# Replacing a fixed stage order by a list scheduler, with one pool of PSUM banks and smaller first loads

## The chip, the cores and the metric

One core of a Trainium2 chip. The metric is the time on the device in microseconds (us) of one execution. Five instruction queues matter: TensorE (PE in the profile, its weight loads as PEld), VectorE (DVE), ScalarE (ACT), GpSimd (POOL, which here mostly issues loads) and SyncE (SP, which issues the stores).

Two things about the times have to be known from the start. First, the profile records the clock that was *granted* to TensorE, as a share of full speed. It is either 1.0 or 0.5, and it changes several times in one execution. Second, the changes fall on a grid of 3.41 us whose phase against the kernel is chance. On one core the states "fast" and "slow" of a run only say whether it was within 1.5% of the fastest of its kernel. The mean clock that is quoted for a run or a stretch counts the time before the run's first clock record as full clock. Ratios called "ratio of the fast runs" are the mean time of one kernel's fast runs over that of the other's of the same rounds, so they are not quite the ratio of the medians that are quoted beside them.

## The reference, cut to what matters

Eight batches of eight heads, 576 tokens, 64 wide. Four heads see the last 32 tokens, four see every fourth of the last 128. The result goes through a soft mixture of experts: every token has logits for 32 slots, softmax over tokens builds the slot inputs, 8 experts of two layers work on 4 slots each, softmax over slots brings the result back.

```python
scores = np.where(masks, scale * q @ k.T, -1e9); attn = softmax(scores) @ v   # local windows
x = attn.transpose(0, 2, 1, 3).reshape(4608, 512)
logits = x @ phi                                   # 4608 x 32
slot_input = softmax(logits, axis=0).T @ x         # 32 x 512, over all tokens of all batches
slot_out[e] = relu(slot_input[e] @ w1[e]) @ w2[e]  # needs every batch
out = softmax(logits, axis=1) @ slot_out           # 4608 x 512, f32
```

The experts need all batches, so the program has three main parts in a row: attention with routing (batch by batch), experts, output.

## The kernel before

A "group" is the four heads of one type in one batch: 16 groups. The stages of a group, by the letters that the code and this text use:

- A: 4 pieces of 18 transposes of q, k, v (96x64 blocks) into one PSUM bank; ScalarE copies Q, K, V out of it.
- B: 6 transposes of v back to token order; VectorE copies.
- S: 6 score matmuls (4 pieces per group); ScalarE takes exp, VectorE multiplies by the mask.
- P: 12 matmuls of probabilities with v (2 pieces); VectorE divides by the row sum into XB.
- once per batch: X (4 pieces of 6 transposes of XB), L (8 logits matmuls of 288 columns), exp on ScalarE, E (12 small matmuls of 32 columns), I (48 small matmuls of 32 columns that sum up the slot inputs).

```python
    ps2 = [A(nc.psum_tensor(f"ps2_{i}", [128, 2, 512], F32)) for i in range(2)]   # two pairs of banks
    ps1 = [A(nc.psum_tensor(f"ps1_{i}", [128, 512], F32)) for i in range(3)]      # three single ones
    psA = A(nc.psum_tensor("psA", [128, 512], F32))                               # the slot sums
    # ... each stage takes the next buffer of its ring
    def st_A(g, r):
        # ...
                    i_ = t.transpose(pbf[64 * hx:64 * hx + 64, NR * i:NR * i + NR],
                                     stg_x[s][0:NR, 2 * typ + hx, c, :], ident[0:NR, 0:NR])
    # ...
    for step in range(-1, 2 * B + 2):     # the fixed order; g = step, b = g // 2, odd = g % 2
        if on: st_B(g, 0); st_S(g, 0, 0)
        if nx: st_A(g + 1, 0)
        if on: st_S(g, 0, 1)
        if nx: st_A(g + 1, 1)
        if pr: st_P(g - 1, 1)
        if on: st_B(g, 1)
        if odd and 0 <= b - 1 < B: st_L(b - 1)
        if not odd and 0 <= b - 1 < B: st_X(b - 1, 2); st_X(b - 1, 3)
        if on: st_S(g, 1, 0)
        if nx: st_A(g + 1, 2)
        if odd and 0 <= b - 1 < B: st_E(b - 1)
        if on: st_S(g, 1, 1)
        if nx: st_A(g + 1, 3)
        if on: st_P(g, 0)
        if odd and 0 <= b - 1 < B: st_I(b - 1)
        if odd and 0 <= b < B: st_X(b, 0); st_X(b, 1)
        # ... then the loads of batch b + 3 and of one expert's weights
```

Loads: `load_w1(0)`, then q, k, v of batch 0 for all eight heads, and so on in turn, all from GpSimd's queue.

The softmax here doesn't subtract the row's maximum and nothing guards it: scores larger than these inputs give would overflow.

## Time and profile before

261.67 us median of 2 runs (261.45 to 261.89); the profiled run has a span of 261.6 us.

| stretch | us | TensorE busy | idle |
|---|---|---|---|
| wait for the first q, k, v | 0 to 17.8 | 0 | 17.8 |
| attention and routing | 17.8 to 217.5 | 184.0 | 15.7 |
| experts | 217.5 to 235.0 | 15.2 | 2.3 |
| output | 235.0 to 261.6 | 10.5 | (stores) |

The table comes from this view, the busy time of each engine by stretch. Each line has the stretch in us from the start, its length, then the busy us of PE, PEld, DVE, ACT and POOL with the instruction counts, the mean granted clock, the DMA engines' share and GB/s:

```profile
0.00:17.80 17.80, 0.03 (x2) 0.06 (x3) 0.63 (x10) 1.28 (x1) 14.95 (x41) 1.00 0.91 175
17.80:217.50 199.70, 184.03 (x2848) 150.62 (x2848) 105.09 (x202) 110.84 (x280) 15.69 (x28) 0.64 0.72 142
217.50:235.00 17.50, 15.22 (x174) 7.31 (x173) 2.66 (x7) 1.05 (x3) 0.00 (x0) 0.87 0.00 1
235.00:261.60 26.60, 10.51 (x35) 2.14 (x36) 12.71 (x18) 12.06 (x18) 0.00 (x0) 0.77 0.89 355
```

Attention is bound by TensorE: 92% busy, the others near 55%. But the mean clock of 0.64 is still too kind, as the slice view shows. It cuts the span in 40 slices; PE and DMA are busy tenths, PEclk the granted clock in tenths:

```profile
PE   0027998999899989989998999899888758888700
...
PEclk9999999997557555555575575555555555999955
DMA  6999999999999509998910664178037700007998
```

The nines of PEclk in the first nine slices are an absence of records: the first clock record of this trace is at 58.4 us. What TensorE's clock was is better read from durations. This is the timeline of TensorE alone (start, us, line, operation, tile written <- tiles read, shapes, count), around one of the short spells of full clock, which the records put at 82.27 to 85.68 us:

```profile
83.23 0.57 PE L307 MATMUL ps_1<-ident,stg 96*64 96x96 bf16 x18
83.74 0.73 PE L377 MATMUL ps_0<-VN,PT 128*96 128x65 bf16 x12
84.39 1.63 PE L457 MATMUL psA<-ET,XB 96*64 96x32 bf16 x48
...
89.23 0.93 PE L307 MATMUL ps_0<-ident,stg 96*64 96x96 bf16 x18
90.09 1.17 PE L377 MATMUL ps_1<-VN,PT 128*96 128x65 bf16 x12
...
203.52 1.63 PE L457 MATMUL psA<-ET,XB 96*64 96x32 bf16 x48
```

The same piece A (L307) takes 0.57 us in the spell and 0.93 us outside it; P (L377) takes 0.73 and 1.17 us. Before 58 us they take 0.93 and 1.17 us too, so the clock was at half there. I (L457, 48 matmuls of 32 columns) takes 1.63 us at either clock: at 84.39 us in the spell and at 203.52 us far outside one.

What TensorE waited for, longest first (us in total, times, longest):

```profile
PE ps_0 L307 <- DMA stg<-in_v_dram: 17.8, 1, 17.8
PE ps_1 L398 <- DVE XB L386: 3.3, 4, 1.3
PE ps_1 L333 <- ACT VT L318: 2.6, 4, 1.9
```

### The profile page before, as it was taken

The numbers are of one execution on the slowest core, as the hardware profiler recorded it, in microseconds if no ns is written. First come the engines' busy times: TensorE is split into PE (matmuls) and PEld (weight loads), VectorE is DVE, ScalarE is ACT, GpSimd is POOL, SyncE is SP. The second block draws the span as 40 slices with busy tenths as digits, with TensorE's granted clock in tenths as the row PEclk, the third lists the DMA queues.
The fourth block names the chain that finished last, engine by engine and source line by source line (L and its number), as shares of the span: only waits on it lengthen the run. The fifth ranks groups of instructions, "written<-read, shape, count | busy, mean of one in ns | idle before, by whom it ended". The sixth has DMA issues, their size and how long they took to land.

```text
span 261.6 us, 7056 instructions
## 1 busy us (share of the span) xinstructions
PE 209.8 (80%) x3055; PEld 160.1 (61%) x3056; DVE 121.1 (46%) x237; ACT 125.2 (48%) x302; POOL 30.6 (12%) x68
## 2 busy tenths in 40 slices
PE   0027998999899989989998999899888758888700
PEld 0025787778787867877787878778766734531100
DVE  0001557636644565466366545644664521219900
ACT  1017785565576545645655764456463010008900
POOL 7970300300030022002000000000000000000000
PEclk9999999997557555555575575555555555999955
DMA  6999999999999509998910664178037700007998
GB/s 110 207 219 208 220 209 217 214 215 212 219 198 216 118 4 189 220 219 153 215 37 3 114 113 99 19 148 147 18 38 137 152 0 3 3 0 289 406 404 345
DMA packets 8910, 40.88 MB, mean 156 GB/s; under 512 B 1456, under 2 KB 1456, under 8 KB 6832
## 3 DMA queue, kind: packets, MB, share of 16 engines
q0 software_dynamic: 5760, 30.94, 60.4%
q1 hardware_dynamic: 3120, 9.50, 9.2%
q8 instruction: 24, 0.39, 0.6%
q14 instruction: 6, 0.05, 0.0%
HBM read 61.93 MB, written 9.44 MB: 273 GB/s over the span
## 4 chain that ended last, share of the span: by engine, by line
PE 60%; ACT 10%; DMA 10%; DVE 9%; issue 4%; POOL 2%; POOLq 0%; ACTq 0%
DMA stg<-in_v_dram 10%; PE ps_1 L377 5%; PE psA L457 5%; PE ps_0 L377 4%; PE ps_2 L307 4%; PE ps_0 L307 4%; PE ps_1 L307 3%; PE ps_1 L587 3%; PE ps_0 L352 3%; PE ps_1 L417 3%; PE ps_0 L417 3%; DVE XB L386 3%; DVE w1r L612 3%; PE ps_1 L352 3%; ACT PT L358 3%
## 5 line engine op out<-in xcount | busy, mean ns | idle before, releaser
L307 PE MATMUL ps_0<-ident,stg 96*64 96x96 bf16 x414 | 21.2, 280 | 17.8 <-DMA stg<-in_v_dram 17.8
L358 ACT ACTIVATE PT<-ps_0 128x576 bf16<-128x576 f32 x32 | 21.1, 660 | 26.8 <-PE ps_0 L352 26.7
L358 ACT ACTIVATE PT<-ps_1 128x576 bf16<-128x576 f32 x32 | 21.1, 660 | 25.3 <-PE ps_1 L352 25.3
L361 DVE TENSOR_TENSOR PT<-PT,mask_d 128x576 bf16<-128x576 bf16 x32 | 14.7, 458 | 37.4 <-ACT PT L358 37.4
L307 PEld LDWEIGHTS ps_0<-ident,stg 96*64 96x64 bf16 x414 | 17.0, 162 | 20.7 <-POOL siT L293 17.7
L361 DVE TENSOR_TENSOR PT<-PT,mask_p 128x576 bf16<-128x576 bf16 x32 | 14.7, 458 | 25.8 <-ACT PT L358 25.1
L307 PE MATMUL ps_2<-ident,stg 96*64 96x96 bf16 x396 | 19.8, 275 | 0.2 <-DMA stg<-in_v_dram 0.2
L318 ACT ACTIVATE QT<-ps_0 128x288 bf16<-128x288 bf16 x23 | 10.4, 451 | 18.6 <-PE ps_0 L307 18.6
L377 PE MATMUL ps_1<-VN,PT 128*96 128x65 bf16 x192 | 17.8, 262 | 0.4 <-ACT PT L358 0.4
L377 PE MATMUL ps_0<-VN,PT 128*96 128x65 bf16 x192 | 17.8, 263 | 0.0
L307 PEld LDWEIGHTS ps_2<-ident,stg 96*64 96x64 bf16 x396 | 15.9, 159 | 3.1 <-issue 0.3
L377 PEld LDWEIGHTS ps_1<-VN,PT 128*96 128x96 bf16 x192 | 15.7, 183 | 2.3 <-PE ps_0 L352 0.6
L307 PE MATMUL ps_1<-ident,stg 96*64 96x96 bf16 x342 | 17.0, 274 | 0.0
L337 DVE COPY VN<-ps_1 128x768 bf16<-128x768 bf16 x12 | 6.6, 548 | 22.1 <-PE ps_1 L333 22.1
L377 PEld LDWEIGHTS ps_0<-VN,PT 128*96 128x96 bf16 x192 | 15.8, 184 | 1.6
L386 DVE TENSOR_TENSOR XB<-ps_0,RV 96x768 bf16<-96x768 f32 x16 | 15.3, 954 | 0.6
L386 DVE TENSOR_TENSOR XB<-ps_1,RV 96x768 bf16<-96x768 f32 x16 | 15.3, 953 | 0.6
L226 POOL DMA_DIRECT2D stg<-in_q_dram x8 | 4.4, 553 | 93.1 <-PE ps_1 L307 39.5
L307 PEld LDWEIGHTS ps_1<-ident,stg 96*64 96x64 bf16 x342 | 13.6, 158 | 2.4
L457 PE MATMUL psA<-ET,XB 96*64 96x32 bf16 x384 | 13.0, 217 | 0.6 <-DVE ET L443 0.6
L352 PE MATMUL ps_0<-QT,KT 64*128 64x96 bf16 x192 | 13.3, 267 | 0.0
L352 PE MATMUL ps_1<-QT,KT 64*128 64x96 bf16 x192 | 13.3, 267 | 0.0
(114 smaller groups left out, 377.8 us busy)
## 6 DMA issues: line engine op xcount, KB each, us to landing
out_dram<-w1r SPq DMA_DIRECT2D x18, 512.0 KB, 5.1
w1r<-in_moe_w_dram POOLq DMA_DIRECT2D x8, 1024.0 KB, 21.3
stg<-in_moe_w_dram POOLq DMA_DIRECT2D x6, 1024.0 KB, 8.0
stg<-in_q_dram POOLq DMA_DIRECT2D x8, 576.0 KB, 12.7
stg<-in_k_dram POOLq DMA_DIRECT2D x8, 576.0 KB, 14.8
stg<-in_v_dram POOLq DMA_DIRECT2D x8, 576.0 KB, 17.0
w2r<-in_moe_w_dram POOLq DMA_DIRECT2D x2, 1024.0 KB, 21.7
phi_st<-in_moe_phi_dram SPq DMA_DIRECT2D x1, 64.0 KB, 2.0
```

Of the source, the lines that this page charges most:

```text
L307: i_ = t.transpose(pbf[64 * hx:64 * hx + 64, NR * i:NR * i + NR], stg_x[s][0:NR, 2 * typ + hx, c, :], ident[0:NR, 0:NR])
L318: op("act", lambda ac, d=d, t=t: ac.activation(d, pv[:, t], ACTF.Copy), r=[pb], **{"w" if r == 0 else "a": [bd[par]]})
L337: op("dve", lambda vv: vv.tensor_copy(vt[:, half, :, :, 0:64], pbf[:, 0:768].rearrange("p (m x d) -> p m x d", m=NB, x=2)), r=[pb], w=[vb[ ...
L352: i_ = t.matmul(sc[:, hx, QB * mm:QB * mm + QB], KT[par][64 * hx:64 * hx + 64, half, QB * m:QB * m + 128], QT[par][64 * hx:64 * hx + 64, h ...
L358: op("act", lambda ac: ac.activation(pt[:], sc[:, :, 0:3 * QB], ACTF.Exp, scale=SCALE), r=[scb], w=[ptb])
L361: op("dve", lambda vv: vv.tensor_tensor(pt[:], pt[:], mk.unsqueeze(1).to_broadcast([128, 2, 3 * QB]), AluOp.mult), r=[b_mask[typ]], w=[ptb])
L377: i_ = t.matmul(po[0:QB, hx, 65 * m:65 * m + 65], pts[m // 3][0][:, hx, QB * (m % 3):QB * (m % 3) + QB], vt[:, half, m, hx, 0:65], start=T ...
L386: op("dve", lambda vv: vv.tensor_tensor(xd, pv[:, :, :, 0:64], rv[:].unsqueeze(3).to_broadcast([QB, 2, NB, 64]), AluOp.mult), r=[pob, rvb] ...
L417: i_ = t.matmul(lg[:, hf, 0:288], phi_pad[:, c].rearrange("p j i -> p (j i)"), XT[:, c, 288 * hf:288 * hf + 288], start=c == 0, stop=c == 3)
L457: i_ = t.matmul(psA[64 * typ:64 * typ + 64, 32 * c:32 * c + 32], x_, et[:, NB * typ + m, :], start=(b == 0 and m == 0 and c == 0), stop=(b ...
L587: i_ = t.matmul(sp_[32 * j:32 * j + 32, :], hT[:, hi, cc, j, :], w2v[e][:, cc, :], start=(hi == 0 and cc == 0), stop=(hi == 1 and cc == 7))
L612: op("dve", lambda vv, o=o, po=po: vv.tensor_scalar(ost[:, o % NO, 1, :], po[:, 1, :], rtok[:, 2 * o + 1:2 * o + 2], None, op0=AluOp.mult) ...
```

## The change

The intent: let a program, not a person, decide the order. Every operation becomes a task with an engine, an assumed duration and a due time. A list scheduler places tasks one by one: per engine it takes those that could start within 0.14 us of the earliest, and of those the one due first. The durations given for TensorE are those of the full clock (0.5 us for a piece A that takes 0.86 at half). PSUM becomes one pool of seven banks that the scheduler hands out. Loads are by four heads, and those of batch 0 go ahead of all weights. The setup memsets move from GpSimd to VectorE. The matmuls, evictions and bytes are the same.

```diff
+def place(tasks, banks, filler):
+    # ... ready lists per engine, bank occupancy, modelled start times
+            for t in lst:
+                st = t0
+                for p in t.preds:
+                    # ...
+                    st = max(st, p.end + lat)
+                for h in t.ps:
+                    if h.banks is None:
+                        f = find(h)              # a free bank, or two neighbours
+                        # ...
+                        st = max(st, f[0])
+                if e == "pe" and t.mode != last_mode[0]:
+                    st += 0.13
+                cands.append((st, t))
+            m = min(c[0] for c in cands)
+            st, t = min((c for c in cands if c[0] <= m + 0.14), key=lambda c: (c[1].due, c[1].idx))
 # ...
-    ps2 = [A(nc.psum_tensor(f"ps2_{i}", [128, 2, 512], F32)) for i in range(2)]
-    ps1 = [A(nc.psum_tensor(f"ps1_{i}", [128, 512], F32)) for i in range(3)]
+    NBK = 7
+    psum = A(nc.psum_tensor("psum", [128, NBK, 512], F32))
     psA = A(nc.psum_tensor("psA", [128, 512], F32))
 # ...
+        for typ in range(2):                      # loads by groups of four heads
+            for t, src in enumerate((q, k, v)):
+                load(lambda g, t=t, src=src, typ=typ: g.dma_start(
+                    stg[32 * t:32 * t + 32, s, 4608 * typ:4608 * typ + 4608].rearrange(...),
+                    src[b, 4 * typ:4 * typ + 4].rearrange(...)), due, 1.45, s_in[s][typ], ...)
 # ...
-        op("pe", pe, r=[b_id, b_in[s]], w=[pb])
+        op("pe", pe, r=[b_id, b_in[s][typ]], ps=[h], dur=0.5, due=due, mode="col")
 # ... every other stage likewise: a duration and a due time; I in two halves
-    for step in range(-1, 2 * B + 2):
-        # ... the fixed order
+    plan = {0: [("w1", 0)], 1: [("w1", 1)], 2: [("w1", 2)], 3: [("w1", 3)], 4: [("w1", 4)],
+            5: [("w1", 5), ("w1", 6)], 6: [("w1", 7), ("w2", 0), ("w2", 1)],
+            7: [("w2", e) for e in range(2, 8)]}
+    for b in range(B):
+        load_qkv(b, -26.0 + b)
+        # ... weights by plan, then the stages of both groups, then X, L, E, I
 # ...
+    for t in place(tasks, NBK, filler):
+        emit(t)
```

## The prediction

> **What bounds the kernel now.** Four stretches, read from the timeline and the stretch table.
> (a) 0 to 17.8 us: TensorE waits for the first batch of q, k, v (waits by engine: 17.8 us on the DMA of v), because 1 MB of w1 and all eight heads are queued ahead; the DMA engines moved about 213 GB/s.
> (b) 17.8 to 217.5 us: attention and routing. TensorE is the limit: 183.9 us busy of 199.7, while ScalarE and VectorE are near 60%. A batch takes 23.4 to 24.8 us, of which TensorE is idle only 1.1 to 1.3 us. The idle time is 9.0 us between 34 and 206 us; the rest is the first fill and the last batch's serial chain (idle 5.9 us from 196 to 218).
> (c) 217.5 to 235 us: the expert layers.
> (d) 235 to 261.6 us: 9.4 MB of output at 350 to 400 GB/s, DMA bound; the evictions keep 0.73 us per 512 KB, faster than the DMA.
>
> TensorE runs at half clock in most of (b). The slice table's 0.9 before 58 us only means that there is no record: 18 input transposes take 0.86 us there, 0.50 us at the full clock. The clock rose four times, each time after a window holding the logits matmuls (8 of 288 columns, about 1.95 us), and fell one window (3.4 us) later. The Trainium skill, "TensorE: Matmul & The Clock Gate", Part 4, says that transposes do not count as busy for the clock; the trace agrees: 104.5 to 129.3 us was 96% busy at clock 0.50.
>
> **What the change does.** The same matmuls, evictions and bytes. The order comes from a scheduler whose durations are those of the full clock (0.50 us for the transposes that take 0.86). Setup memsets move from GpSimd to VectorE. Banks 2x2+3 become a pool of seven. The first loads are half size and precede w1.
>
> **Costs on the critical path.**
> - Start: 0.88 MB instead of 2.8 MB before the first transpose: 4.2 us at 213 GB/s instead of 13.3; TensorE starts at 8.3 us instead of 17.8: -9.5.
> - Idle in (b): 15.9 us falls to about 8 (first fill 2, final chain 4.5, rest 1.5): -8.
> - TensorE's 183.9 us of work stays: the clock stays half for most of it, because the work that counts stays about a third of each window. A few more logits windows may warm: -2, with mode switches equal (six score matmuls of 41 ns hold 0.35 us, so about 0.1 each; the skill's "TensorEngine Tiling (Array Packing)", Tiling Modes, says that a mode change drains the engine).
> - Expert layers: row sums leave the path: -0.5. Output: unchanged.
> - More and smaller DMAs: GpSimd issues 24 more of 0.55 us, hidden. Loads need about 145 us and fit.
>
> Sum with the cold clock: 261.7 - 20 = 242. If the denser order keeps the clock full for most of attention (my chance: one in five), TensorE drops to about 6.5 us per group, the bound becomes ScalarE (7 to 8 us per group) and the loads, and the time falls to 195 to 215 us. Between both I put 238 us, range 212 to 248. Chances: faster 0.95, same 0.04, slower 0.01.
>
> **What would show it.** First transpose at 8 to 9 us; TensorE over 96% busy between 15 and 190 us; transposes still 0.86 us for 18; clock records mostly 0.5 with short spells of 1.0; expert layers begin near 198 us; output 25 us long and DMA bound.
>
> **What would make it wrong.** The clock staying full (much faster). The order, planned with half the real TensorE times, making engines wait in order for late work. More mode switches from finer interleaving. The second batch's load arriving late, since the pool of loads is in order.

## The result, and the profile after

214.32 us median of 2 runs (213.49 and 215.16); ratio of the fast runs 0.8397, with an interval of 0.8231 to 0.8563. Six more runs on another chip gave 214.36 us (210.93 to 216.56). The kernel before was unlucky in its first two runs: in 29 later ones it took 244.7 to 263.1 us (mean clock of the whole run from 0.83 down to 0.68). Where both ran, the medians were 255.54 and 214.36 us, a ratio of 0.839. The fast runs alone (2 of 11, and 3 of 6) have means of 244.75 and 212.8 us, a ratio of 0.87.

The same view by stretch, with the borders of the new kernel:

```profile
0.00:9.20 9.20, 0.00 (x0) 0.01 (x1) 4.81 (x31) 1.28 (x1) 7.87 (x19) 1.00 0.77 135
9.20:167.20 158.00, 139.38 (x2884) 117.13 (x2884) 99.76 (x203) 109.83 (x280) 28.23 (x53) 0.89 0.94 191
167.20:185.20 18.00, 15.08 (x138) 6.59 (x138) 2.27 (x6) 1.04 (x3) 0.00 (x0) 0.83 0.01 2
185.20:211.80 26.60, 9.82 (x35) 2.60 (x36) 11.94 (x18) 10.69 (x18) 0.00 (x0) 0.79 0.89 355
```

The start is 8.6 us shorter and the attention stretch 41.7 us; experts and output have not moved. The gain in attention is not idle time: idle is 18.6 us (158.0 less 139.4) against 15.7 before. It is TensorE's busy time, 139.4 us against 184.0, for the same 3055 matmuls of the whole program (36 row-sum matmuls of the expert part now fall in this stretch).

```profile
PE   0279999997899899799888999977946788899000
...
PEclk9999999999979999859998569997875569999955
DMA  5999999999999999999999998976940000069998
```

The first clock record is now at 36.8 us and says 1.0, and the nines of the middle are real. The timeline of TensorE shows it, cold at 26.7 and warm at 45 us:

```profile
26.70 1.17 PE L524 MATMUL psum<-VN,PT 128*96 128x65 bf16 x12
...
42.77 1.63 PE L619 MATMUL psA<-ET,XB 96*64 96x32 bf16 x48
...
45.37 0.57 PE L446 MATMUL psum<-ident,stg 96*64 96x96 bf16 x18
45.87 0.73 PE L524 MATMUL psum<-VN,PT 128*96 128x65 bf16 x12
```

And what TensorE waited for:

```profile
PE psum L446 <- DMA stg<-in_v_dram: 9.2, 1, 9.2
PE psum L446 <- issue: 2.9, 4, 1.3
PE psum L524 <- DVE PT L505: 2.5, 5, 1.8
PE psum L496 <- ACT KT L456: 1.6, 1, 1.6
```

The clock is not up all the time: the records of attention show spells of 20.5, 27.3, 20.5, 20.5 and 6.8 us at 1.0, with 3.4 to 10.2 us at 0.5 between them. So the question is why the clock is up so much longer, and whether that is all.

### What a window has to hold

The records change only on the 3.41 us grid, so each window can be set against the clock of the next. I counted the matmul work in each window as its moving columns at 2.4 GHz, whatever the clock really was (2.4 GHz is from the Trainium skill, "TensorE: Matmul & The Clock Gate", Part 1; the trace agrees: logits matmuls of 288 columns start 240 ns apart at half clock, that is, 1.2 columns per ns). A matmul that fills only 64 rows or 64 columns of the array (A, S, I) counts half; that weight is an assumption, chosen because it fits. Every matmul counts, transposes too. This is worked out from the trace, not a view of the profile; us of counted work by stage:

```
kernel  window  clock  work  next  of which
before   55.0   0.5    1.60  1.0   A .28 B .24 L .96 S .12
before   58.4   1.0    1.23  0.5   A .44 E .16 I .18 P .32 S .12
before   78.9   0.5    1.44  1.0   A .36 L .96 S .12
before   82.3   1.0    1.25  0.5   A .36 E .16 I .28 P .33 S .12
after    33.4   0.5    1.42  1.0   A .05 B .64 S .24 X .48
after    36.8   1.0    2.18  1.0   A .66 L .96 P .43 S .12
after    40.2   1.0    1.36  1.0   B .32 E .16 I .19 P .22 S .24 X .24
after    43.6   1.0    1.84  1.0   A .58 B .32 I .13 P .32 S .24 X .24
after    47.0   1.0    1.70  1.0   A 1.38 P .32
after    50.4   1.0    2.26  1.0   A .78 B .64 S .36 X .48
after    53.8   1.0    1.39  0.5   A .86 L .08 P .32 S .12
```

Over the 98 whole windows of attention in both traces, the rule "the next window is at full clock if this one holds 1.44 us of counted work" is wrong 10 times. Left out of the count, transposes make it wrong 21 times at the best line. The window at 33.4 us holds 24 transposes of B and X, 12 score matmuls and next to nothing else, and the clock rose. With its 1.42 us it is itself one of the 10 windows that the rule gets wrong, as is the one at 40.2 us, which kept the full clock with 1.36 us: near the line the rule doesn't decide. The halving carries much of it. In a recount of all the traces (575 windows after a first record, each matmul put into the window in which it starts), the best line with the halving is wrong 48 times. With every matmul counted whole it is wrong 143 times, no better than saying "as this window" (140).

By this count the old order at half clock stays under the line, and a denser order can stay over it. A batch holds 8.8 us of counted work (my sum over its stages). At half clock the old kernel needs 24.8 us for a batch, 1.21 us per window, which is under the line, so only a window that catches L whole rises. In the changed kernel a batch of 15.4 to 20.4 us (from L to L in the profiled run, all but the last; the clock is at 0.72 to 1.0 in them) holds 1.48 to 1.95 us per window on average, over the line. In the old order the window after each rise was the one with E and I, 1.22 to 1.26 us in all four spells, and it always fell back. In the first spell of the changed kernel the scheduler has S, B, X and S between E (40.9 us) and I (42.8 us), and L is followed by A and P at once.

Theory ("clock"): the order earns the clock, and the clock is the gain. Rival ("order"): the order, the pool of banks or the loads save time themselves, and the clock only follows.

### The profile page after: what moved, and what is told of

The parts are those of the page before. It is cut to its first block, busy times and chain, and to the rows that moved or that the text cites. A ratio compares the mean times of both kernels' runs of the same rounds, so it can differ in the third digit from the quotient of the medians.

```text
span 211.8 us, 6954 instructions
## 1 busy us (share of the span) xinstructions
PE 164.3 (78%) x3055; PEld 126.3 (60%) x3056; DVE 118.8 (56%) x258; ACT 122.8 (58%) x302; POOL 36.1 (17%) x71
## 4 chain that ended last, share of the span: by engine, by line
PE 54%; DVE 15%; ACT 14%; issue 6%; DMA 3%; POOL 1%; DVEq 0%; POOLq 0%
PE psum L446 9%; PE psum L524 7%; PE psum L470 6%; PE psum L496 6%; PE psA L619 6%; DVE w1r L762 5%; PE psum L551 5%; PE psum L574 5%; PE psum L734 4%; ACT QT L456 4%; ACT KT L456 3%; PE psum L679 3%; DMA stg<-in_v_dram 3%; ACT VT L456 3%; DVE XB L536 3%
## 5 line engine op out<-in xcount | busy, mean ns | idle before, releaser
L502 ACT ACTIVATE PT<-psum 128x576 bf16<-128x576 f32 x64 | 42.5, 675 | 26.3 <-PE psum L496 25.1
L446 PE MATMUL psum<-ident,stg 96*64 96x96 bf16 x1152 | 38.3, 232 | 12.2 <-DMA stg<-in_v_dram 9.2
L446 PEld LDWEIGHTS psum<-ident,stg 96*64 96x64 bf16 x1152 | 33.3, 129 | 15.7 <-issue 13.7
L456 ACT ACTIVATE QT<-psum 128x288 bf16<-128x288 bf16 x64 | 30.8, 482 | 11.9 <-PE psum L446 11.9
L456 ACT ACTIVATE VT<-psum 128x288 bf16<-128x288 bf16 x64 | 31.1, 488 | 1.3 <-PE psum L446 1.3
L536 DVE TENSOR_TENSOR XB<-psum,RV 96x768 bf16<-96x768 f32 x32 | 30.5, 954 | 1.1
L456 ACT ACTIVATE KT<-psum 128x288 bf16<-128x288 bf16 x64 | 31.0, 484 | 0.0
L524 PE MATMUL psum<-VN,PT 128*96 128x65 bf16 x384 | 26.8, 227 | 3.4 <-DVE PT L505 2.5
L524 PEld LDWEIGHTS psum<-VN,PT 128*96 128x96 bf16 x384 | 24.1, 144 | 6.4 <-DVE PT L505 3.6
L474 DVE COPY VN<-psum 128x768 bf16<-128x768 bf16 x32 | 17.7, 552 | 15.9 <-PE psum L470 15.8
L496 PE MATMUL psum<-QT,KT 64*128 64x96 bf16 x384 | 21.2, 225 | 4.2 <-ACT KT L456 1.6
L496 PEld LDWEIGHTS psum<-QT,KT 64*128 64x128 bf16 x384 | 11.1, 102 | 10.2 <-ACT VT L456 2.3
L470 PEld LDWEIGHTS psum<-ident,VT 128*128 128x128 bf16 x192 | 13.6, 111 | 2.8 <-ACT VT L456 0.4
```

Of the source, the lines that this page charges most:

```text
L446: i_ = t.transpose(o[64 * hx:64 * hx + 64, NR * i:NR * i + NR], stg_x[s][0:NR, 2 * typ + hx, c, :], ident[0:NR, 0:NR])
L456: op("act", lambda ac, d=d, t=t: ac.activation(d, bf(h)[:, 0:9 * NR].rearrange("x (c t h p) -> x t h p c", c=9, t=3, h=2)[:, t], ACTF.Copy ...
L470: i_ = t.transpose(o[:, 128 * m:128 * m + 128], VT[par][:, half, QB * m:QB * m + 128], ident[:, :])
L474: op("dve", lambda vv: vv.tensor_copy(vt[:, half, :, :, 0:64], bf(h)[:, 0:768].rearrange("p (m x d) -> p m x d", m=NB, x=2)), w=[vb], ps=[ ...
L496: i_ = t.matmul(sc[:, hx, QB * mm:QB * mm + QB], KT[par][64 * hx:64 * hx + 64, half, QB * m:QB * m + 128], QT[par][64 * hx:64 * hx + 64, h ...
L502: op("act", lambda ac: ac.activation(pt[:], f32(h)[:, :, 0:3 * QB], ACTF.Exp, scale=SCALE), w=[ptb], ps=[h], dur=0.54, due=due + 0.2)
```

## The experiments

Twelve kernels ran, in three calls of four, each call on one chip with runs of the kernel before beside them. All gave right results. One earlier build stopped before the chip: the scheduler ran out of banks, because a dummy task of `a_fill` took a bank long before its partner could follow; tying it to the P matmuls before it cured that.

### First call: loads, dummy work, old order (kernel before: 251.8 us, 251.1 to 263.1)

**b_loads.** The kernel before, with only the loads changed.

```diff
-    load_w1(0)
+    load_qkv(0)          # by four heads, semaphores per half; then load_w1(0)
-        op("pe", pe, r=[b_id, b_in[s]], w=[pb])
+        op("pe", pe, r=[b_id, b_in[s][typ]], w=[pb])
```

> The kernel before, with only the loads changed: by groups of four heads, the first batch ahead of w1. Both theories expect the start term alone: first transpose at about 9.2 us as in the changed kernel instead of 17.8, also no wait for the second batch at 31.7 us. Clock theory: order and sparse windows are as before, so the clock stays at half for most of attention (record mean of that stage 0.50 to 0.60), batch period 23.4 to 24.8 us, total about 252 us (249 to 256). If the loads by four heads were what let the clock rise, the total would be below 235 us.

Measured: 252.07 us median, but one of the four runs took 643.24 us (see the last section), and it was the profiled one. The fast three are at 250.8 to 252.9 us at a clock of 0.70 to 0.71. That equals the fast runs of before in the call (ratio 1.0006, 0.9931 to 1.008), but those had a clock of 0.77. The seven runs of before at 0.70 to 0.72, all on other chips, took 260.1 to 262.0 us. So at equal clock the loads are worth about 9 us by this estimate, as much as the start term (first transpose at 9.3 us). They do not raise the clock.

**b_fill.** The kernel before plus 8 dummy matmuls per batch in its sparse spots.

```diff
+    def fill(t, bank, n):
+        for _ in range(n):
+            i_ = t.matmul(bank[:, 0:512], ident[:, :], mask[0][:]...[:, 0:512], start=True, stop=True)
 # st_X, for the first of each pair, ahead of the wait for XB:
+            op("pe", lambda t: fill(t, t1, 3), r=[b_id, b_mask[0]], w=[pb])
 # st_E, ahead of its matmuls:
+            fill(t, t1, 2)
```

> The kernel before, order, banks and loads untouched, with 8 dummy matmuls (128x128x512) per batch added on TensorE in the sparse spots: 2 ahead of the slot-weight transposes, 3 ahead of each of two pairs of token transposes, where TensorE waits for VectorE. About 1.7 us of extra work per batch at the full clock, 3.4 at half. Clock theory (a window of 3.41 us with at least about 1.4 us of matmul work, counted at the full clock, earns the full clock for the next): the extra work lifts the sparse windows over the line, the clock stays at 1.0 for most of attention, batch period 17 to 19 us, total 215 to 232 us, faster than before with more work. Rival (the order and the idle time it removes are what counts, the clock follows something else): slower, 262 to 285 us.

Measured: 243.5 us (242.95 to 247.82), ratio of the fast runs to before 0.969 (0.9638 to 0.9742), at a clock of 0.87 to 0.90. Its slowest run (247.82 us) is faster than the fastest of before in the call (251.06 us). More work, and faster: the direction of the clock theory, and the rival's "slower" is out. But the size is a miss. A batch took 20.1 to 22.1 us, not 17 to 19:

```profile
18.00:200.70 182.70, 157.68 (x2912) 122.93 (x2912) 102.85 (x203) 108.82 (x280) 15.56 (x28) 0.87 0.78 155
```

Busy time fell from 184.0 to 157.7 us in spite of the dummies, but idle rose from 15.7 to 25.0 us. At the full clock the old order waits more.

**b_loads_fill.** Both edits.

> Both edits together: old stage order, old bank rings, new loads, dummies. Clock theory: 205 to 222 us, near the changed kernel's 214, without any scheduler. Rival: 252 to 275 us.

Measured: 235.8 us (231.02 to 238.71), clock 0.87 to 0.91. Also a miss: the clock is at the level of the changed kernel, and 21 us are still lacking against its median on another chip. The clock alone is not enough.

**a_fixed.** The changed kernel, with TensorE, ScalarE and VectorE held to the old stage order.

```diff
+    line = {e: [t for t in tasks if t.eng == e] for e in ("pe", "act", "dve")}
+            if e in line:
+                lst = [t for t in lst if t is line[e][0]]
 # and the stages are created by the old loop
```

> The changed kernel with its new loads, setup on VectorE and pool of seven banks, but TensorE, ScalarE and VectorE in the old fixed stage order. Clock theory: the sparse windows after the logits are back, so the clock falls after each rise: attention's mean clock 0.50 to 0.65, total 246 to 256 us, like the run with the new loads alone. If the pool of banks is what does it: 214 to 225 us with the clock up.

Measured: 241.81 us (235.26 to 245.63). The four runs follow their clock: 0.829, 0.779, 0.748 and 0.735 gave 235.3, 239.9, 243.7 and 245.6 us. The median lies 4 us below the range expected, because the clock rose more often than expected:

```profile
9.40:200.40 191.00, 172.26 (x2848) 141.43 (x2848) 105.80 (x207) 110.03 (x280) 28.03 (x53) 0.70 0.78 158
```

The clock of 0.70 in attention is still far from the 0.89 of the changed kernel, so the pool of banks with the new loads and setup does not hold it up in the old order. In one batch of this trace the clock was at 0.95, without any dummy: it took 18.8 us, with 3.4 us idle, where the three batches at 0.57 took 23.4 to 23.8 us.

### Second call: the order at equal clock (kernel before: 255.5 us, 244.7 to 261.3)

**after_again.** The changed kernel.

> The changed kernel itself, unaltered, for its spread: the phase of the 3.41 us windows against the kernel is chance, and the kernel before spread over 251 to 263 us by its granted clock (0.78 to 0.69). Clock theory: the changed kernel stays high, 208 to 222 us, and its time falls as its recorded clock rises.

Measured: 214.36 us (210.93 to 216.56), clock 0.85 to 0.88.

**a_banks.** The changed kernel, with the scheduler kept to the old split of banks.

```diff
-        for b0 in range(banks - h.n + 1):
+        for b0 in ((0, 2) if h.n == 2 else (4, 5, 6)):
```

> The changed kernel, but the scheduler may use the banks only as the kernel before did: pairs from banks 0 to 3, single banks from 4 to 6. If the pool of seven is needed for the order that works: over 222 us. Clock theory, with banks a side matter: within 3% of the changed kernel of the same call, clock within 0.04 of it.

Measured: 218.86 us (215.67 to 223.22), clock 0.80 to 0.86. Within 3% as expected. Giving up the free pool costs about 4 us. But the scheduler then also finds another order for TensorE (the sequence in the trace differs), and the clock is 0.03 lower, so I cannot say how much of the 4 us is the pool itself.

**a_fixed_fill and a_fill.** The old stage order and the scheduler's order, both with the new loads, the pool and the same 8 dummies (in `a_fill` the scheduler places them).

> Old fixed stage order with new loads, the pool of seven and the 8 dummy matmuls per batch. If only the clock were missing in the old order: equal to the changed kernel, 210 to 220 us, at a clock of 0.88 or more. If the order also saves time at the full clock (the earlier pair of old order, old banks and dummies took 231 to 239 us at 0.87 to 0.91): 226 to 240 us.

> The changed kernel with the same 8 dummy matmuls per batch, placed by its scheduler. Same work and nearly the same clock as the run with the old order and dummies, so the difference of the two is what the order is worth at the full clock: expected 12 to 20 us. Against the changed kernel: the clock rises to 0.93 or more in attention, which pays for the dummies: 206 to 218 us.

Measured: 234.49 us (229.81 to 235.57) against 211.96 us (209.64 to 214.77). The fast runs of both have the same clock, 0.915 and 0.917, and means of 229.9 and 211.1 us. So the order itself is worth 19 us near the full clock. The lines of attention of the two traces, `a_fixed_fill` and then `a_fill`:

```profile
9.40:183.30 173.90, 147.94 (x2912) 117.02 (x2912) 104.42 (x207) 108.63 (x280) 28.05 (x53) 0.94 0.86 173
```

```profile
8.90:167.00 158.10, 144.46 (x2948) 113.44 (x2948) 100.67 (x203) 110.88 (x280) 28.59 (x54) 0.91 0.94 191
```

Attention is 15.8 us shorter, and idle is 26.0 us in the old order and 13.6 us in the new one, at nearly the same work. That is where the order pays. At half clock TensorE was so slow that ScalarE and VectorE were nearly always ready (idle 1.1 us of a 24.8 us batch), and there was little for an order to win. Against the changed kernel of the same call, `a_fill` is 2.4 us faster by the medians, 1.1%. The clock with the dummies is 0.90 to 0.93, and they give most of what it is worth back in their own time.

### Third call: transposes, weights, planned durations (kernel before: 260.1 us, 252.0 to 262.0)

**b_fill_T.** `b_fill` with each dummy matmul of 512 columns replaced by four transposes of 128.

```diff
-            i_ = t.matmul(bank[:, 0:512], ident[:, :], mask[0][:]...[:, 0:512], start=True, stop=True)
+            for j in range(4):
+                i_ = t.transpose(bank[:].bitcast(BF16)[:, 128 * j:128 * j + 128],
+                                 mask[0][:]...[:, 128 * j:128 * j + 128], ident[:, :])
```

> The kernel before with the dummies as in the earlier run on it, but each 512-column matmul replaced by four 128x128 transposes: the same number of streamed columns. This tests the step of the prediction that transposes do not count for the clock. If they do not: the clock stays where the kernel before has it (0.69 to 0.78) and the dummies only cost time: 258 to 275 us. If they count like matmuls: clock 0.86 to 0.90 and 240 to 249 us, as with the matmul dummies (243.5 us at 0.89).

Measured: 249.38 us (241.89 to 252.03), at a clock of 0.85 to 0.92, where the kernel before had 0.70 to 0.78 in the same call. The median is 0.4 us above the range expected, and the clock is about as expected. The slowest of its six runs is level with the fastest of eleven of before (252.0 us), with more work to do. Transposes count for the clock. In attention of its profiled run the clock was at 0.85, where the kernel before had 0.64:

```profile
18.10:205.90 187.80, 160.40 (x3104) 136.97 (x3104) 103.40 (x202) 108.94 (x280) 15.41 (x28) 0.85 0.76 151
```

**a_wlate and a_wlate_fill.** The expert weights moved behind the batches in the queue of loads, without and with the dummies.

```diff
-    plan = {0: [("w1", 0)], 1: [("w1", 1)], 2: [("w1", 2)], 3: [("w1", 3)], 4: [("w1", 4)],
-            5: [("w1", 5), ("w1", 6)], 6: [("w1", 7), ("w2", 0), ("w2", 1)],
-            7: [("w2", e) for e in range(2, 8)]}
+    plan = {0: [], 1: [], 2: [("w1", 0)], 3: [("w1", 1)], 4: [("w1", 2)], 5: [("w1", 3)],
+            6: [("w1", 4)], 7: [("w1", e) for e in (5, 6, 7)] + [("w2", e) for e in range(8)]}
```

> The changed kernel with the expert weights moved behind in the queue of loads: one w1 between batches from the third on, the other eleven after the last batch. In the changed kernel the halves of the seventh and eighth batch land at 95 to 122 us and TensorE waits for them; with this the eighth lands at about 95 us. If the loads pace the changed kernel once the clock is up: main stage 158 us falls to 138 to 148 us, clock 0.90 or more in it, total 192 to 204 us. If they do not: within 2% of 214 us.

> The same with the 8 dummy matmuls per batch. Where the loads no longer open gaps, the clock should hold by itself, so the dummies are nearly pure cost: 0 to 5 us above the run without them. If the clock still falls without them: up to 6 us below.

Measured: 215.12 us (212.65 to 218.98) and 214.82 us (212.42 to 217.21). My reason for `a_wlate` has fallen. The last batch's data did land earlier (101.9 us instead of 122.1), and the total did not move. So I find no sign that the loads pace the changed kernel. The run is not a pure test of the loads, since the scheduler places them too and with another queue it also gave TensorE another order. Its clock fell to 0.80 to 0.88, and the dummies that raise it to 0.89 to 0.91 cost as much as they bring. Here is attention in `a_wlate`:

```profile
10.80:170.00 159.20, 141.43 (x2884) 120.84 (x2884) 100.25 (x203) 109.64 (x280) 26.43 (x50) 0.83 0.93 188
```

**a_colddur.** The changed kernel, with TensorE's durations in the plan as measured at half clock.

```diff
-        op("pe", pe, r=[b_id, b_in[s][typ]], ps=[h], dur=0.5, due=due, mode="col")
+        op("pe", pe, r=[b_id, b_in[s][typ]], ps=[h], dur=0.9, due=due, mode="col")
 # likewise B .35 -> .66, S .16 -> .25, P .56 -> .93, X .28 -> .5, L 1.0 -> 1.95, E .55 -> .72, I .65 -> .78
```

> The changed kernel, its scheduler given TensorE durations as measured at half clock (0.9 us for 18 input transposes instead of 0.5, and so on). Any valid order runs; if the full-clock durations in the plan are what gives the order its worth, this falls back by 8 us or more (222 to 240 us). If any list-scheduled order does: within 3% of the changed kernel, 208 to 221 us.

Measured: 237.66 us (230.58 to 241.37), clock 0.72 to 0.82, 23 us slower than the changed kernel (which ran on another chip, where before took 255.5 instead of 260.1 us) and as much slower than `a_wlate` on the same chip. It has only one fast run, and that one (230.58 us) is slower than every run of the changed kernel. The first branch holds. In the source nothing but eight numbers of the plan differs; the order that comes out is another:

```profile
9.30:191.20 181.90, 163.69 (x2884) 134.74 (x2884) 101.92 (x203) 113.16 (x280) 28.19 (x53) 0.70 0.82 166
```

Idle is 18.2 us, as in the changed kernel, but busy time is 163.7 instead of 139.4 us. A list schedule as such does not hold the clock up; the order that was planned for the full clock does so for most of attention.

### The counting rule on traces it was not made from

The line of 1.44 us was set on the traces of before and after alone. On the attention windows of the other eleven profiled kernels that have clock records it is wrong for 38 of 517 windows (7%). Saying "as this window" is wrong 114 times, and the rule without transposes, with its own line from the first two traces, 144 times. A recount differs a little with how a matmul on a border is counted: 40 to 55 of 545 windows wrong, with the time before a first record taken as half clock. It is a description, not a mechanism: how much a half-filled array counts is not settled, and a variant with other weights for A, X, S and I was wrong 34 times.

## Why the prediction was right or wrong

The measured 214.3 us lies in the range (212 to 248), near its lower end, and "faster" was given 0.95. But the 238 us was put together from a branch at half clock (242 us) and one at full clock given one chance in five (195 to 215 us), and the branch thought unlikely is what happened. That the time fell into the range is luck: the range took in only the upper end of that branch, 212 to 215 us. The unlikely branch had its mechanism wrong too. It expected TensorE to drop to 6.5 us per group and ScalarE and the loads to become the limit. TensorE still needs 8.7 us per group (139.4 over 16) and is 88% busy in attention, ScalarE is 70% busy, and the loads set no pace that `a_wlate` could show.

| term | predicted, half-clock branch | measured in the traces |
|---|---|---|
| start | -9.5 | -8.6 (17.8 to 9.2) |
| idle in attention | -8 | +2.9 (15.7 to 18.6) |
| TensorE's work in attention | -2 | -44.6 (184.0 to 139.4) |
| experts | -0.5 | +0.5 |
| output | 0 | 0.0 |

- The start was right. Loads by four heads ahead of w1 do that by themselves; `b_loads` has its first transpose at 9.3 us.
- The step that failed: "TensorE's 183.9 us of work stays: the clock stays half for most of it, because the work that counts stays about a third of each window." It rested on the Trainium skill, "TensorE: Matmul & The Clock Gate", Part 4, that transposes do not count as busy for the clock. My evidence for it was a stretch 96% busy at half clock. That evidence was weak: the stretch holds about 1.2 us of counted work per window with transposes counted fully, which is also too little. `b_fill_T` shows that transposes count, and the rise after the window at 33.4 us agrees.
- With them counted, a batch has on average enough work to hold the full clock once it runs at that clock. I did see that a rise always fell back one window later, but I took this for a property of the stage, not of what the old order put into that window.
- The idle term was wrong in sign, for a reason that the runs show: idle belongs to the clock. The old order at the full clock idles 25 to 26 us (`b_fill`, `a_fixed_fill`), and the new order brings this to 14 to 19 us. Against the half-clock kernel it looks like no gain at all.
- The costs were right: 24 more load issues cost TensorE no wait after the first, and the output stays 26.6 us and bound by its stores (355 GB/s in the table above, before and after).
- "Mode switches equal" was nearly right: TensorE changes its tiling 178 times in attention before and 167 times after, counted in the traces. That a change drains TensorE is from the Trainium skill, "TensorEngine Tiling (Array Packing)", Tiling Modes. The page gives no time for it, and no run here measures one; the 0.1 us is the prediction's estimate.

How the 41.7 us of attention divide: the two causes need not add up. At half clock the old order left only 1.1 us of idle time in a batch of 24.8 us, so the order would be worth little there; no run has the new order at half clock, so this is argued and not shown. Near the full clock the order is worth 19 us in the whole program, 15.8 us of them in attention (`a_fixed_fill` against `a_fill`). The old order with the clock raised by dummies alone, `b_fill`, is 17 us shorter in attention than the profiled run of before, which was an unlucky one; by the medians of its call it gains 8 us. The pool of banks is worth about 4 us at most, with what its order and clock bring.

What stays open: why the clock follows this count, and exactly what a half-filled array counts for it; why the clock still falls in some batches of the changed kernel (its lowest batch has a mean of 0.72); and whether an order exists that never falls. None of the variants beat the changed kernel by more than 1.1% in its median.

## What to carry to other kernels

Read the granted clock by windows before costing TensorE: a kernel that is 95% busy at half clock may be able to run most of its time at full clock. What fits here is the matmul work per window, above all in the sparsest window after each rise; no kernel of this case kept the full clock through all of attention. Plan an order with the durations of the state that you want to be in, and spread the small matmuls that keep TensorE busy without doing much. A cheap test for such a state is to add dummy matmuls in the sparse spots: if the kernel gets faster with more work, as `b_fill` did, the clock was a limit.

## What the Trainium skill lacked or had wrong

- "TensorE: Matmul & The Clock Gate", Part 4, says that the full clock does not engage for transposes, which do not count as busy in the same way. Here they count: a window of 24 transposes and 12 score matmuls was followed by the full clock, and dummy transposes raised the old kernel's mean clock from a range of 0.70 to 0.78 to one of 0.85 to 0.92.
- The same page, Part 1, gives a window of about 3.4 us and two clocks, and the trace agrees (spells of 3.41 us and multiples, 1.0 and 0.5). It lacks what "busy" means: TensorE was 96% busy at half clock for a whole batch. What fits here is about 1.44 us of moving columns at 2.4 GHz per window, with half-filled matmuls counted half, right for 93% of 517 windows. One line serves for rising and for staying; fitted apart in a recount they come out at 1.41 to 1.45 and at 1.38 to 1.39 us.
- The same page mentions a clock stuck at a quarter for over 50 us. One run of `b_loads` took 643 us with TensorE 97% busy and no clock record at all: logits matmuls of 288 columns were 652 to 830 ns apart, by turns and in every batch, against 240 ns at half clock, while ScalarE and VectorE were busy as long as ever (130 and 126 us). That is about 0.39 columns per ns, where a quarter of 2.4 GHz would be 0.6. The page has no case that long or that slow; it was seen once and has no cause here.
- The same page says that the phase of the windows varies from run to run and that the cost of the ramp is below 1% of a typical span. That figure is for the ramp alone. For a kernel whose clock falls back again and again, the phase shifts far more: the kernel before took 244.7 to 263.1 us, 7%, mostly in step with the mean clock (0.83 down to 0.68; the correlation over 29 runs is -0.92).
